# Broadcasts and output tiles in one DMA issue each, and a load order behind a gather, in an attention-plus-MLP kernel

## The chip, the core and the metric

The kernel runs on one core of one Trainium2 chip. The metric is the device time of one execution in microseconds (us); the median of several runs is compared. The engines have short names: PE is TensorE, DVE is VectorE, ACT is ScalarE, POOL is GpSimd, SP is SyncE. SP computes nothing here; it issues DMAs, one after the other, and waits on semaphores before each where it must.

## What is computed

Cosine attention for 8 batches, 12 heads, 448 positions and 64 columns per head, and then a feed-forward layer with the gate h * cos(h):

```
q_n = q / (norm(q) + 1e-06);  k_n = k / (norm(k) + 1e-06)
attn = softmax(q_n @ k_n.T / tau);  attn_out = attn @ v        # (8, 12, 448, 64)
x = attn_out, heads side by side                               # (3584, 768)
h = x @ w_in                                                   # (3584, 2048)
out = (h * cos(h)) @ w_out                                     # (3584, 768)
```

## The kernel before

**Units, pairs, batches.** The 96 heads are taken in pairs of two (48 pairs, g), three pairs make a unit (16 units, u), and two units a batch (8 batches). For each pair, q and k are loaded in float32 ("load u p", L589, two DMAs), squared, summed and normalised, scaled to bf16 (POOL, L668) and transposed, from pair 9 on by a DMA transpose ("T", L685). PE then makes the scores (L719, L727), ACT their exponentials (L734), and PE multiplies them with v and with ones (L760 to L793), so that each pair leaves unnormalised outputs and sums of exponentials.

**From sums to xT.** For pairs in the "direct" list the reciprocals are made on ACT. For the others, 34 pairs in 13 units, `chain` (L884) does it: a gather of the sums from SBUF to SBUF in two DMAs (L888), a sum and a reciprocal on 128 partitions (DVE, L900 and L903), a "spread" of the result to a scratch tensor in DRAM (L904), and a broadcast from there into RB, each half of the 128 partitions by its own DMA (L906): 64 partitions read the same row of n x 448 floats, n the number of pairs. POOL multiplies outputs by RB into xT (L910).

**The feed-forward part.** Per batch, `m1` multiplies xT (six chunks, one for each pair) by w_in in 16 steps of six matmuls (L918); ACT and DVE make h * cos(h) (L947, L949) into gT, which has room for two batches. The second product runs in 28 tiles of 128 tokens (L1016, the last ones L1045); its fills are spread between the scores of the next batch, where PE would wait for ACT. DVE copies each tile to one of three buffers osb (L983), and SP writes it to DRAM in two DMAs of 64 partitions (L987). A tile's token p of segment h goes to row `row + 7 * p`; 28 tiles over eight batches of 448 tokens make tiles 3, 10, 17 and 24 straddle two batches.

**Order.** PE's order is written out by hand: PLAN holds scripts in which `s24.2` is a block of scores, `a`, `b`, `c` the parts of attention, `f5` five fills and `m4` a block of the feed-forward part, and "given" holds the fills of some pairs. The other engines' orders come from a planner (`Program.arrange`), which plays the program with a cost for each operation and a due time, and takes what is ready and due first. `dma` gives each issue a cost and a number of descriptors from the table ISSUE (L525), and a pad, time that the planner adds after landing. "queue" in PLAN holds pairs of issues whose order on SP is fixed. Waits are set from the order found.

So an instruction waits in its engine's order for the ones before it: SP for the inputs of an issue, DVE for a gather's landing.

Of the kernel before, what the change touches and what calls it, by code (L numbers as in the profile page):

```python
# [13 lines left out]
PLAN = {  # L14
    "apart": 1,
    "ahead": (1, 2),
    "hurry": {},
    "rush": {},
    "swapped": {},
    "script": {19: """  # L20
        s19.0 f5 s19.1 f4 s19.2 f6 s19.3 f6 a18 f4 b18 s20.0 c18 c19
        s20.1 f2 a19 f2 b19 s20.2 f4 s20.3 f4 a20 s21.0 f4 s21.1 f4 b20 c20 s21.2 f6 s21.3 f6 o201 m2 c21
# [9 lines left out]
        s37.3 f4 s38.0 f4 s38.1 f4 s38.2 f4 s38.3 f4 a37 f2 b37 s39.0 c37 c38 s39.1 a38 f3 b38 f1 s39.2 f3 s39.3 f3 m5 c39  # L32
        a39 f4 s40.0 b39 f4 s40.1 f4 s40.2 f2 s40.3 f2 s41.0 s41.1 f4 s41.2 f5 s41.3 f5 a40 f2 b40 s42.0 c40 c41
        s42.1 a41 f3 b41 f1 s42.2 f4 s42.3 f4 s43.0 f4 s43.1 f4 s43.2 f5 s43.3 f5 a42 f2 b42 s44.0 c42 c43
        s44.1 f2 a43 f2 b43 s44.2 f5 s44.3 f7 a44 s45.0 f5 s45.1 f5 s45.2 f6 b44 c44 s45.3 f10 o012 m6 f6 s46.0 f12 a45 s46.1 b45 f4 c45 s46.2 f3 s46.3 f4
        """},
    "after": (0, 1, 2, 0, 1, 2, 0, 1),
    "queue": (("bcast13", "out18"), ("bcast9", "out11"), ("bcast11", "out15"),
              ("spread13", "T46"), ("spread9", "T34"), ("spread11", "T40")),
    "last": ((0,), (1,), (2,)),  # L40
    "folded": (0, 1, 2, 3),
    "grid": {2: (16, 5, 6), 3: (11, 3, 4), 4: (8, 2, 3)},
# [6 lines left out]
    "v3": (7, ("xa", 2, 0)),  # L49
    "late4": {2: (7, "T9")},  # L50
    "power": (2,),
    "late": 0.5,
    "mixed": (3, (3, 0, 1, 2, 0, 1, 2, 0), (2, 3, 4, 0, 1, 5)),
    "turned": 9,
    "first": (3, 1, 2, 0, 3, 1, 2, 0),
# [14 lines left out]
    "u5": ("gather2", "gather2", "gather2"),  # L70
    "tail": 192,
    "twin": 4,
    "given": {13:(0,0,2,3),16: (4, 0, 5, 2), 22:(1,2,5,6), 34: (12, 4, 5, 6), 46: (12, 4, 3, 4), 47: (4, 0, 5, 0)},
    "roots": (3, (14, 0), (10, 0)),
    "lead": {33: 5, 45: 6, 12: 13, 21: 13},
    "vloads": {3: [(4, "x6"), (5, "x6")], 4: [(6, "x11")], 5: [], 6: [(7, "x15"), (8, "x15")]},
# [338 lines left out]
def bass_cosine_attention__then__act_gcu_kernel(  # L415
# [9 lines left out]
    B, NH, S, D = q.shape  # L425
    DM = NH * D
# [3 lines left out]
    UH = 2 * UP  # L430
    NG = UP * NU
    PB = NG // B
    NB = 7
    NT3 = NB // 2
    BP = S // NB
# [23 lines left out]
    def sbs(name, n, shape, dt):  # L459
        return [sb("%s%d" % (name, i), shape, dt) for i in range(n)]  # L460

    def ps(name, shape, dt):
# [20 lines left out]
    osb = sbs("osb", 3, [128, DM], F32)  # L483
# [12 lines left out]
    scr = nc.dram_tensor("scr", (NU, UH * S), F32)  # L496
# [11 lines left out]
    RBv = [t.ap().rearrange("p (g s) -> p g s", g=UP) for t in RB]  # L508
# [13 lines left out]
    MH = HW / 2400.0 + 0.0025  # L522
    HALF = 0.096

    ISSUE = {"load": (0.62, 128), "gather": (0.64, 128), "spread": (0.4, 128), "bcast": (0.62, 64),  # L525
             "out": (0.62, 64), "T": (1.27, 1024)}

    def dma(eng, fns, reads, writes, sem, bulk=0.0, label="", behind=None, weight=1.0, pad=0.0):
        took, descs = 0.75, 0
        for y in ISSUE if eng == "SP" else ():  # L530
            if label.startswith(y):
                took, descs = ISSUE[y]
        o = P.op(eng, lambda e: [f(e) for f in fns], reads, writes, cost=took * len(fns), dma=sem, bulk=bulk, label=label)
        o.nd, o.descs, o.lead = len(fns), descs * len(fns), 0.3 if label[0] == "T" else 0.0
        o.weight, o.pad = weight, pad
        if behind is not None:
            P.order_only(behind, o)
        return o
# [3 lines left out]
    def act(fn, reads, writes, cols, table=None, aps=0, label="", bias=0.0):  # L542
        o = P.op("ACT", fn, reads, writes, cost=0.165 + cols / 1200.0 + 0.09 * aps, label=label, bias=bias)
        if table is not None:
            if last_table[0] is not None:
                P.order_only(last_table[0], o)
            last_table[1].append(o)
        return o
# [9 lines left out]
    def dve(fn, reads, writes, cycles, lock=False, label="", bias=0.0):  # L558
        return P.op("DVE", fn, reads, writes, cost=0.15 + cycles / 960.0, lock=lock, label=label, bias=bias)

    def pool(fn, reads, writes, cost, label="", bias=0.0):
        return P.op("POOL", fn, reads, writes, cost=cost, lock=True, label=label, bias=bias)
# [321 lines left out]
    def chain(u):  # L884
        i, b = u % 2, u // 2
        n = sum(UP * u + p not in PLAN["direct"] for p in range(UP))
        w = SPR // UP * n
        dma("SP", [lambda e, r=r: e.dma_start(  # L888
            sums[i].ap()[:, w * r : w * r + w],
            bass.AP(xu, (32 * r * 5 + 3 + i) * UP * S, [[64 * 5 * UP * S, 2], [w, 64], [1, w]]))  # L890
            for r in range(2)], [("xs", i, p) for p in range(n)], [("sums", i)], "sums%d" % i, 0.7,
            "gather%d" % u, pad=0.0 if u in PLAN["power"] else PLAN["late"])
        r = rcp[i].ap()[:, 0:w]
        parts = sums[i].ap()[:, 0 : 2 * w].rearrange("p (r x) -> p r x", r=2)
        if u in PLAN["power"]:
            pool(lambda e: e.tensor_tensor(r, parts[:, 0], parts[:, 1], ALU.add), [("sums", i)], [("rcp", i)], 0.23, label="sum")
            pool(lambda e: e.tensor_tensor(r, r, bass.AP(cst, 2, [[4, 128], [0, w]]), ALU.pow), [("rcp", i), "cst2"], [("rcp", i)],
                 0.05 + 0.166 * w, label="recip")
        else:
            dve(lambda e: e.tensor_reduce(out=r, in_=sums[i].ap()[:, 0 : 2 * w].rearrange("p (r x) -> p x r", r=2),  # L900
                                          axis=mybir.AxisListType.X, op=ALU.add), [("sums", i)], [("rcp", i)], 2 * w,
                label="sum", bias=PLAN["rush"].get(u, 0.0))
            dve(lambda e: e.reciprocal(r, r), [("rcp", i)], [("rcp", i)], 8 * w, label="recip", bias=PLAN["rush"].get(u, 0.0))  # L903
        dma("SP", [lambda e: e.dma_start(bass.AP(scr, u * UH * S, [[w, 128], [1, w]]), r)],  # L904
            [("rcp", i)], [("scr", u)], "scr", 0.02, "spread%d" % u).bias = PLAN["hurry"].get(u, 0.0)
        dma("SP", [lambda e, a=a: e.dma_start(  # L906
            RBv[i][64 * a : 64 * a + 64, 0:n], bass.AP(scr, u * UH * S + a * n * S, [[0, 64], [1, n * S]])) for a in range(2)],
            [("scr", u)], [("RB", i, p) for p in range(n)], "RB%d" % i, 3.4 * n / UP, "bcast%d" % u, None, 2.4, 0.5).bias = PLAN["hurry"].get(u, 0.0)
        for p in range(n):
            pool(lambda e, p=p: e.tensor_tensor(xTv[b % 2][:, UP * i + p, :], xuv[:, u % 3, p, :], RBv[i][:, p, :], ALU.mult),  # L910
                 [("RB", i, p), ("xa", u % 3, p)], [("xT", b % 2, UP * i + p)], 1.1, label="x%d" % (UP * u + p))
# [42 lines left out]
    def segments(t):  # L954
        segs = []
        for h in range(2):
            x = 128 * t + BP * h
            segs.append((BP * h, x // S * S + x % S // BP))
        return segs
# [17 lines left out]
    def m2_drain(t, hf, name, po, w):  # L977
        o, n, ends = t % 3, w[1] - w[0], t == B * S // 128 - 1
        dst, keys = osb[o].ap()[:, w[0] : w[1]], [("osb", o, y) for y in range(2)]
        if ends and w[1] == DM:  # L980
            act(lambda e: e.activation(dst, po[:, 0:n], ACT.Copy, bias=0.0), name + [("osb", o, 0)], [("osb", o, hf)], n, label="osb%d" % t)
        else:
            dve(lambda e: e.tensor_copy(dst, po[:, 0:n]), name, [("osb", o, hf)], n, label="osb%d" % t)  # L983
        if not ends and hf == 0:
            return
        c0, c1 = w if ends else (0, DM)
        fns = [lambda e, p0=p0, row=row: e.dma_start(  # L987
            bass.AP(out.tensor, row * DM + c0, [[NB * DM, BP], [1, c1 - c0]]), osb[o].ap()[p0 : p0 + BP, c0:c1]) for p0, row in segments(t)]
        for x, eng in enumerate(("SP", "ACT") if ends and hf else ("SP",)):
            dma(eng, fns[x : x + 1] if ends and hf else fns, [("osb", o, hf)] if ends else keys, [], "last" if x else "out%d" % o,  # L990
                n / DM if ends else 1.0, "out%d" % t, None, 1.0)

    def gates(t, f, m):
        par = sorted({(x // S) % 2 for x in (128 * t, 128 * t + 127)})
# [139 lines left out]
    def unit_done(g):  # L1134
        u = g // UP
        if g > PB and not direct(g - 1) and (g % UP == 0 or direct(g)):
            chain((g - 1) // UP)
        if g % UP == 0:
            if g > PB and (u <= 3 or u % 2 == 0):
                for x in range(UP if u + 2 < NU else 0):  # L1140
                    load(u + 2, x, x + 1, behind=find("bcast%d" % (2 if u == 4 else u - 1)) if u > 3 else
                         find(PLAN["u5"][x]) if u == 3 else None)
            if g > PB:
                for x, y in PLAN["vloads"].get(u, [(u + 2, "x%d" % (g - 1 if u % 2 == 0 else g - 4))]):
                    load_v(x, find(y))
# [156 lines left out]
    if not direct(NG - 1):  # L1302
        chain(NU - 1)
# [47 lines left out]
```

## Time and profile before

| what | us |
|---|---|
| median of 3 runs (range) | 421.33 (420.74 to 423.37) |
| the profiled execution | 421.37 |
| its span, first to last instruction | 419.6 |
| PE busy in the span | 410.8 |
| SP's issues of broadcasts (L906), first to last start | 79.2 to 370.8 |
| median landing of a 336 KB broadcast DMA, from its issue | 4.8 |
| median landing of a 192 KB output DMA, from its issue | 3.6 |
| granted PE clock | 1.000 |

The span counts from the first instruction, and all places in time below are microseconds from it. A row of the profile's groups names line, engine, operation and tiles, output before input. A wait is put down to what ended it. In windows, the columns after the five engines' busy times are the granted clock, the DMA share (the mean busy share of the core's 16 DMA engines) and GB/s. DMA packets moved 63.61 MB in the span, most of it in the first two thirds.

### The profile page before, as it was taken

To read this page: it belongs to the slowest core of one execution; us is meant where nothing else is said; L and a number is where in the kernel's file an instruction comes from. 1 tells how busy PE (TensorE), PEld (TensorE's weight loads), DVE (VectorE), ACT (ScalarE), POOL (GpSimd) and SP (SyncE) were. 2 spreads that over 40 slices of the span, in tenths; PEclk is the share of its full clock that TensorE was granted. 3 is DMA by queue.
4 is the path that set the end of the run, shared out by engine and by line. 5 is a ranking of instruction groups with operands and counts; after the bars stand their busy time and mean duration, and the time that the engine had idled before them with its cause. 6 is when DMAs were issued, how large, how long until landed. Compare 5 with 4: busy or idle time off the path is not lost.

```text
span 419.6 us, 13577 instructions
## 1 busy us (share of the span) xinstructions
PE 410.8 (98%) x6077; PEld 237.0 (56%) x6077; DVE 189.1 (45%) x250; ACT 271.9 (65%) x363; POOL 242.7 (58%) x193
## 2 busy tenths in 40 slices
PE   8899999999999999999999999999999999999997
PEld 3454556655556555665566555665566655565565
DVE  4564744456653277124752087213862244223421
ACT  5897578984986646877498556776498745703500
POOL 4999977989862694838864783908857320020000
PEclk9999999999999999999999999999999999999999
DMA  8999999979957998779867993969937720141023
GB/s 186 248 253 226 207 225 171 229 176 195 141 109 142 201 208 195 114 160 218 174 104 133 219 244 76 143 114 208 243 90 122 167 67 2 43 120 38 2 65 86
DMA packets 80254, 63.61 MB, mean 152 GB/s; under 512 B 44996, under 2 KB 75204, under 8 KB 80196
## 3 DMA queue, kind: packets, MB, share of 16 engines
q1 hardware_dynamic: 61988, 50.06, 56.8%
q0 software_dynamic: 18048, 12.59, 20.1%
q8 instruction: 48, 0.79, 0.8%
q10 hardware_dynamic: 160, 0.10, 0.1%
q14 instruction: 10, 0.08, 0.1%
HBM read 54.98 MB, written 11.13 MB: 158 GB/s over the span
## 4 chain that ended last, share of the span: by engine, by line
PE 84%; DMA 5%; ACT 4%; POOL 3%; DVE 2%; issue 1%; SPq 0%; ACTq 0%; DVEq 0%; POOLq 0%
PE MP L1016 25%; PE SC L918 18%; PE AV L918 10%; PE SC L719 6%; DMA sums<-xu 4%; PE AV L767 4%; PE MP L1045 4%; PE SC L1045 3%; PE AV L793 2%; ACT PX L734 2%; PE SC L767 2%; PE AV L760 2%; PE MP L918 2%; POOL qks L668 1%; ACT cosb L947 1%; DVE gT L949 1%
## 5 line engine op out<-in xcount | busy, mean ns | idle before, releaser
L734 ACT ACTIVATE PX<-SC 128x896 bf16<-128x896 f32 (+1 forms) x166 | 132.6, 828 | 25.5 <-PE SC L719 16.8
L1016 PE MATMUL MP<-W,gT 64*64 64x384 bf16 x2816 | 142.1, 323 | 0.9 <-DVE qkT L706 0.6
L1016 PEld LDWEIGHTS MP<-W,gT 64*64 64x64 bf16 x2816 | 79.0, 107 | 36.0 <-PE MP L1016 4.2
L668 POOL TENSOR_TENSOR qks<-raw,rn 128x896 bf16<-128x896 f32 (+1 forms) x48 | 79.8, 1678 | 28.5 <-ACT rn L660 27.9
L918 PE MATMUL SC<-xT,W 128*128 128x448 bf16 x468 | 94.9, 353 | 0.0
L947 ACT ACTIVATE cosb<-SC,cst 128x896 f32<-128x896 f32 x39 | 39.1, 1006 | 57.0 <-PE SC L918 55.1
L629 POOL TENSOR_TENSOR sq<-raw 128x896 bf16<-128x896 f32 x44 | 73.5, 1689 | 4.4 <-DMA raw<-in_q_dram 2.5
L910 POOL TENSOR_TENSOR xT<-xu,RB 128x448 bf16<-128x448 f32 x34 | 37.8, 1137 | 60.5 <-DMA RB<-scr 60.5
L918 PEld LDWEIGHTS SC<-xT,W 128*128 128x128 bf16 x468 | 45.5, 98 | 42.8 <-ACT xu L847 0.6
L949 DVE TENSOR_TENSOR gT<-SC,cosb 128x896 bf16<-128x896 f32 x39 | 42.3, 1088 | 37.5 <-ACT cosb L947 36.1
L918 PE MATMUL AV<-xT,W 128*128 128x448 bf16 x264 | 56.7, 353 | 0.0
L983 DVE COPY osb<-MP 128x384 f32<-128x384 f32 x50 | 25.7, 551 | 64.8 <-PE MP L1016 54.2
L636 DVE TENSOR_REDUCE n<-sq 128x14 f32<-128x896 bf16 (+2 forms) x49 | 51.2, 1057 | 5.9 <-ACT sq L627 5.2
L719 PE MATMUL SC<-qkT 64*64 64x448 bf16 x504 | 45.6, 356 | 0.6 <-ACT PX L734 0.4
L918 PEld LDWEIGHTS AV<-xT,W 128*128 128x128 bf16 x264 | 25.6, 98 | 24.2 <-ACT xu L847 0.3
L947 ACT ACTIVATE cosb<-AV,cst 128x896 f32<-128x896 f32 x22 | 22.1, 1006 | 23.6 <-PE AV L918 20.7
L949 DVE TENSOR_TENSOR gT<-AV,cosb 128x896 bf16<-128x896 f32 x22 | 23.9, 1087 | 15.2 <-ACT cosb L947 15.2
L603 POOL DMA_DIRECT2D va<-in_v_dram x32 | 21.9, 689 | 7.0 <-DMA raw<-in_q_dram 4.3
L877 POOL TENSOR_TENSOR xT<-xu,RB 128x448 bf16<-128x448 f32 x8 | 9.1, 1134 | 29.1 <-ACT RB L873 29.1
L850 DVE COPY xu<-AV 128x896 f32<-128x896 f32 x13 | 14.2, 1091 | 21.2 <-PE AV L783 14.3
L734 ACT ACTIVATE PX<-AV 128x896 bf16<-128x896 f32 (+1 forms) x26 | 21.1, 812 | 2.5 <-PE AV L719 1.7
L719 PEld LDWEIGHTS SC<-qkT 64*64 64x64 bf16 x504 | 14.5, 105 | 14.4 <-ACT PX L734 6.1
(95 smaller groups left out, 430.4 us busy)
## 6 DMA issues: line engine op xcount, KB each, us to landing
raw<-in_k_dram SPq DMA_DIRECT2D x48, 224.0 KB, 6.1
raw<-in_q_dram SPq DMA_DIRECT2D x48, 224.0 KB, 6.9
out_dram<-osb SPq DMA_DIRECT2D x54, 192.0 KB, 3.6
va<-in_v_dram POOLq DMA_DIRECT2D x32, 192.0 KB, 7.8
RB<-scr SPq DMA_DIRECT2D x18, 336.0 KB, 4.8
W<-in_moe_w_in_dram POOLq DMA_DIRECT2D x4, 768.0 KB, 14.7
W<-in_moe_w_out_dram POOLq DMA_DIRECT2D x4, 768.0 KB, 19.4
RB<-scr SPq DMA_DIRECT2D x6, 224.0 KB, 3.7
```

The costliest lines, as they stand in the source:

```text
L629: pool(lambda e, x=x, y=y: e.tensor_tensor(y, x, x, ALU.mult), src_, dst, 0.1 + n * 1.78e-3, label="sq%d.%d" % (u, p)).pad = LATE if u > 1 ...
L636: dve(lambda e, w=w: e.tensor_reduce(out=n2v[i][:, 2 * p : 2 * p + 2, w], in_=sqv[p][:, :, w, :], axis=mybir.AxisListType.X, op=ALU.add), ...
L668: f = lambda e, s0=s0, s1=s1: e.tensor_tensor(qksv[i][:, p, s0:s1].rearrange("p s h d -> p h s d"), rawv[i][:, h, s0:s1, :], bass.AP(rn[i] ...
L719: m = e.matmul(ph[BP * o : BP * o + BP, a, 0:S], t[r, c - 1 + (NT3 + 1) * o, 0:BP], t[r, :, BP : 2 * BP], start=True, stop=True)
L734: act(lambda e: e.activation(PHv[j] if c == 0 else PXv[j][:, c - 1], ph[:, :, 0:n], ACT.Exp, scale=1.0 / TAU), keys, [("PX", j, c)], 2 * n ...
L910: pool(lambda e, p=p: e.tensor_tensor(xTv[b % 2][:, UP * i + p, :], xuv[:, u % 3, p, :], RBv[i][:, p, :], ALU.mult), [("RB", i, p), ("xa", ...
L918: t = e.matmul(ph[:, a, 0:S], W1v[:, order[c], 128 * n : 128 * n + 128], xTv[b % 2][:, order[c], :], start=(c == 0), stop=(c == NKC - 1))
L947: act(lambda e, ph=ph, cz=cz: e.activation(cosv[cz], ph[:, :, 0:S], ACT.Sin, bias=cst.ap()[:, 0:1], scale=1.0), names(gi) + ["cst0"], [("c ...
L949: dve(lambda e, ph=ph, cz=cz, gi=gi: e.tensor_tensor(gTv[:, 2 * gi : 2 * gi + 2, S * (b % 2) : S * (b % 2) + S], ph[:, :, 0:S], cosv[cz], ...
L983: dve(lambda e: e.tensor_copy(dst, po[:, 0:n]), name, [("osb", o, hf)], n, label="osb%d" % t)
L1016: r = e.matmul(POH[b][x : x + 64, 0:HW], gTv[k, y, col + x : col + x + 64], W2v[k, y, HW * b : HW * b + HW], start=(y == 0 and h == 0), st ...
L1045: r = e.matmul(po[:, 0 : w[1] - w[0]], gTv[:, y, col : col + 128], W2v[:, y, w[0] : w[1]], start=(y == 0), stop=(y == NF - 1))
```

## The change

It makes one DMA of two in two places. The broadcast into RB becomes one DMA over 128 partitions, whose source names the two rows outermost. An output tile whose two segments are neighbouring rows of one batch becomes one DMA, whose destination names the two rows outermost; that holds for 23 of the 28 tiles. The planner is told of it (ISSUE, `descs`). "queue" gets three entries: the loads of unit 9 are issued after the gather of unit 6. The pad after a gather, 0.5 for all units but one, becomes 1.0, 1.2 and 1.0 for units 9, 11 and 13. Two orders of PE change by a few fills: those of pair 13, and `f12 a45` becomes `a45 f12`.

In the order that results, SP has the same issues with fewer DMAs. Gather 6 stands ahead of the six load DMAs of unit 9 and behind tile 5; tile 4 stands ahead of transpose 21 rather than behind it. On DVE, sums and reciprocals of units 6, 10, 11, and some neighbours of theirs, move by one or two places. POOL issues the load of unit 15's v six places later, behind the squares of that unit.

```diff
-        s44.1 f2 a43 f2 b43 ... m6 f6 s46.0 f12 a45 s46.1 b45 f4 c45 s46.2 f3 s46.3 f4
+        s44.1 f2 a43 f2 b43 ... m6 f6 s46.0 a45 f12 s46.1 b45 f4 c45 s46.2 f3 s46.3 f4
...
-              ("spread13", "T46"), ("spread9", "T34"), ("spread11", "T40")),
+              ("spread13", "T46"), ("spread9", "T34"), ("spread11", "T40"),
+              ("gather6", "load u9 p0"), ("gather6", "load u9 p1"), ("gather6", "load u9 p2")),
...
-    "late": 0.5,
+    "late": {9: 1.0, 11: 1.2, 13: 1.0},
...
-    "given": {13:(0,0,2,3),16: (4, 0, 5, 2), ...
+    "given": {13: (0, 0, 3, 2), 16: (4, 0, 5, 2), ...
...
-    ISSUE = {..., "bcast": (0.62, 64),
+    ISSUE = {..., "bcast": (0.62, 128),
...
-            "gather%d" % u, pad=0.0 if u in PLAN["power"] else PLAN["late"])
+            "gather%d" % u, pad=0.0 if u in PLAN["power"] else PLAN["late"].get(u, 0.5))
...
-        dma("SP", [lambda e, a=a: e.dma_start(
-            RBv[i][64 * a : 64 * a + 64, 0:n], bass.AP(scr, u * UH * S + a * n * S, [[0, 64], [1, n * S]])) for a in range(2)],
+        dma("SP", [lambda e: e.dma_start(
+            RBv[i][:, 0:n].rearrange("p g s -> p (g s)"), bass.AP(scr, u * UH * S, [[n * S, 2], [0, 64], [1, n * S]]))],
...
+        rows = [row for p0, row in segments(t)]
+        whole = not ends and rows[1] == rows[0] + 1
+        if whole:
+            fns = [lambda e: e.dma_start(bass.AP(out.tensor, rows[0] * DM, [[DM, 2], [NB * DM, BP], [1, DM]]), osb[o].ap())]
...
-                n / DM if ends else 1.0, "out%d" % t, None, 1.0)
+                n / DM if ends else 1.0, "out%d" % t, None, 1.0).descs *= 1 + whole
```

## The prediction

> **What bounds the kernel now.** I read the page first, then the list of DMA issues, the windows, SyncE's timeline, and the waits. The page says that TensorE is the bound and the DMA engines are not, though they are full in the first two thirds:
>
> ```profile
> PE 410.8 (98%) x6077; PEld 237.0 (56%) x6077; DVE 189.1 (45%) x250; ACT 271.9 (65%) x363; POOL 242.7 (58%) x193
> ...
> DMA  8999999979957998779867993969937720141023
> ```
>
> TensorE idles 8.8 us of 419.6, so shorter issues can win very little. The DMA row is a mean over 16 engines, and it hides how one transfer is spread over them. That is what this change alters. The list of DMA issues shows it (size each, median us to landing):
>
> ```profile
> out_dram<-osb SPq DMA_DIRECT2D x54, 192.0 KB, 3.6
> ...
> RB<-scr SPq DMA_DIRECT2D x18, 336.0 KB, 4.8
> ...
> sums<-xu SPq DMA_DIRECT2D x18, 10.5 KB
> scr<-rcp SPq DMA_DIRECT2D x9, 10.5 KB, 1.5
> ```
>
> Only the gathers (sums<-xu, L888) have no landing time. It is given where an issue leaves sixteen landing marks: 22 output issues left 352 marks, 14 gathers left 42, three each. The gather's source pattern has two rows outermost, [[.., 2], [w, 64], [1, w]]; all others have 64 or 128. Windows with one kind of transfer in flight say the same (last columns: granted clock, DMA share, GB/s; first the gathers of unit 15, then the broadcasts of unit 14, then output tile 20):
>
> ```profile
> 364.00:364.90 0.90, 0.90 (x24) 0.45 (x20) 0.00 (x0) 0.15 (x1) 0.00 (x0) 1.00 0.14 12
> 340.00:342.00 2.00, 2.00 (x13) 1.04 (x11) 1.48 (x2) 1.20 (x2) 0.00 (x0) 1.00 1.04 280
> 359.30:360.50 1.20, 1.20 (x38) 0.78 (x28) 0.00 (x0) 0.95 (x2) 0.00 (x0) 1.00 0.99 261
> ```
>
> A share of 0.14 of sixteen is 2.2 engines (packets overlap a little), a share of 1 is all. In the packet records the two gathers issued at 333.35 are 256 packets in exactly two chains. So a gather runs on two engines, and both gathers on the same two. Next, the path of a reciprocal, from SyncE's timeline (start, us: gather, spread, broadcasts), and who waits at its end:
>
> ```profile
> 333.35 1.19 SPq L888 DMA_DIRECT2D sums<-xu  x2
> 336.96 0.35 SPq L904 DMA_DIRECT2D scr<-rcp  x1
> 338.41 1.15 SPq L906 DMA_DIRECT2D RB<-scr  x2
> ```
> ```profile
> POOL xT L910 <- DMA RB<-scr: 60.5, 8, 13.0
> ```
>
> POOL's products feed xT, which the first matmul block of each batch reads (here blocks 2 and 3, in the chain of waits):
>
> ```profile
> 143.53 1.24 PE SC L918 x6
> ...
> 190.46 1.25 PE AV L918 x6
> ```
>
> Unit 7's broadcast landed at 189.98, and its first product ended at 191.19; block 3 wants it at 192.68. There is 1.5 us of slack. TensorE's order is fixed, so a later broadcast stops it.
>
> **The broadcast in one issue (13 times).** It removes 13 issues of 0.55 us (1.15 for two) from SyncE, which idles between its issues: worth nothing. But its source is now [[n*448, 2], [0, 64], [1, n*448]], two rows outermost, the gather's form. I take it that it runs on two engines, which then carry 64 rows of 5376 B each instead of 8. Per row the fastest tenth of the packet records took 206 ns; the quiet window gives 280/16 = 17.5 GB/s per engine, 307 ns. So a broadcast of three pairs keeps two engines for 13.2 to 19.7 us, of two (3584 B) 9.0 to 13.1, of one 4.7 to 6.6. I take the fast ends: 307 ns came with sixteen engines reading the same 5 KB, now two do. Before, issue to last landing was 5.4 us (338.41 to 343.78); alone it becomes 1.3 to the first packet + 13.2 + 0.7 = 15.2.
>
> **The output tile in one issue (23 of 28).** It also removes issue time that hides nothing. The destination is [[768, 2], [5376, 64], [1, 768]], two rows outermost, so 64 rows of 3072 B per engine: 7.7 us at the fastest tenth (121 ns), 8.1 at the median of all records (126), 12.1 at the window's 261/16 GB/s. I take 8.1. Four tiles that straddle batches and the last keep two issues.
>
> The Trainium skill, page "DMA: Bandwidth & Descriptors", section "Why a DMA increments its semaphore by 16 and not by 1", says that the hardware path looks at the slowest dimension above 1 of source and destination and uses the largest number of engines up to 16 that divides both. The gather's marks agree; for a two-row DRAM side no run here shows it. By the same page's ~27 GiB/s per engine (Specifications), an estimate of a three-pair broadcast is 11.9 us and of a tile 6.8, and the sum below would be some 45 us smaller. The section "Bandwidth" of that page says to batch into larger DMAs, which would speak for the change and gives the sixteen-engine rival's time.
>
> **The two engines as a queue.** All other DMAs of SyncE also use these two engines, and packets of a queue are served in order there. Loads, transposes, spreads and gathers therefore wait behind broadcasts and tiles. Per lane the rest costs at the fast records: a unit's loads 48 x 74 ns = 3.5 us, its v 48 x 60 ns = 2.9, a transpose 56 x 18 ns = 1.0, a pair of gathers 1.1. Where a cycle's last reciprocal path is exposed, the lane idles up to 6.4 us (338.41 - 333.35 + 1.3). Cycles run from one block's wait for its last broadcast to the next's:
> Block 2 to 3 (46.9 us of TensorE): loads of 8 and 9 7.0, v 8.7, five transposes 5.0, gathers 2.2, tiles 5 to 8 32.4, broadcasts 13.2 + 9.0, idle 6: 83.5, so +36.6.
> Block 3 to 4 (46.9): 7.0 + 5.8 + 7.0 + 2.2, tile 9 and straddling 10 9.1, 26.4, idle 5: 62.5, +15.6.
> Block 4 to 5 (49.4): 7.0 + 5.8 + 6.0 + 2.2, tiles 11 to 14 32.4, 26.4, idle 6: 85.8, +36.4.
> Block 5 to 6 (47.2): 7.0 + 5.8 + 6.0 + 2.2, tiles 15 to 17 17.2, 26.4, idle 6: 70.6, +23.4.
> Block 6 to 7 (43.4): 1.0 + 2.2, tiles 18 to 21 32.4, 13.2 + 9.0, idle 8: 65.8, +22.4.
> Up to block 2: +5 where block 1 waits for unit 2's broadcast behind tile 0, +19 where T21, spread 5 and broadcast 5 (9.0) stand behind broadcast 4 (13.2) and tile 4 (8.1): +24. End: tile 26, behind 25, lands some 6 us later: +5.8.
> Sum +164.2.
>
> **Loads of unit 9 behind gather 6, pads, script.** The chain of waits has the one stall that this aims at:
>
> ```profile
> 149.04 12.90 DMA sums<-xu
> ```
>
> Gather 6, behind six loads, holds VectorE's sum, then gT, then TensorE: a 0.61 us hole in 165 to 170 (4.39 busy). Freed, it saves at most 0.6; squares of unit 9 waited only 0.40 and 0.61 for loads, so loads some 2 us later cost POOL that, and at most 0.6 reaches TensorE by the same route. The loads, tile 6, spread 6 and broadcast 6 queue behind the gather's wait on SyncE, whose inputs are done at 143.2. New pads move a few sums in VectorE's order by one or two places of 1.09 us, beside TensorE. POOL issues unit 15's v six operations later (1.34 us of issue, from 294.8 to about 304), and 7.8 us of landing leave over 40 us to its first use at 355.5. The swapped fills change order, not work. Together -0.6 to +0.6, taken as 0; the other term covers them.
>
> The profiled execution took 421.37 us, its span 419.6, the median of three 421.33, so 421.4 + 164 = 586.
>
> **Rivals.** (1) Two engines, but slow packets: 4.0 us more per tile (23) and 6.5 per three-pair broadcast (9), 4 per two-pair (3): +162 where all is exposed, some 740. For it: the median 5376 B record is 353 ns; against: fourteen engines are then idle. (2) Only the broadcasts shrink to two engines, because their small dimension is at the source like the gather's, and the tiles' is at the destination, which no row tests. Tiles then cost the lane 1.0: cycles of 55, 55, 57, 56 give +8, +8, +8, +9, with +10 before block 2 and +3 at block 7: 467. (3) The other side, no slower: a DRAM side is split over all sixteen engines whatever its form. Then bytes and packets are as before, and only the 0.6 us hole goes: 420.8. It decides if the issues show sixteen landing marks. Against: the gather. Faster by over 1% needs 4.2 us, half of all of TensorE's idle time, for which no mechanism is in sight.
>
> **Numbers.** Two engines at near the fast rates 0.75, slow packets 0.12, broadcasts alone 0.07, sixteen engines 0.06. Prediction 586. The likeliest case: not below 525, since from tile 0's issue (77.5) the lane has 150 of broadcasts, 178 of tiles and 119 of the rest at the fastest records, with no idle time; up to 660. I give 525 to 700, for part of the slow packets. One per cent, 4.2 us, is about what a measurement of this kernel can tell from no change: slower 0.94, within 0.05, faster 0.01.
>
> **What would show it.** The lists of DMA issues lose the landing times of RB<-scr and of whole tiles; a window with one broadcast alone has a share near 0.13 and 30 to 52 GB/s. POOL's wait for RB<-scr grows from 60 us to well over 100, TensorE's busy share falls to about 70%, with holes ahead of each L918 block and of scores whose transposes are late. Sixteen engines in those windows, or DMA shares near 1, would make the forecast wrong outright; tiles with landing times but broadcasts without mean rival 2.

## The result, and the profile after

| | us |
|---|---|
| changed kernel, median of 5 runs (range) | 624.72 (619.37 to 627.21) |
| kernel before, median of 5 runs (range) | 421.47 (420.74 to 423.37) |
| ratio, with its 95% interval | 1.4797 [1.4763, 1.4831] |
| profiled execution of the changed kernel, and its span | 627.21, 625.3 |
| forecast, and its range | 586, 525 to 700 |

The changed kernel takes half as long again. Line numbers are one higher than before, and five higher behind the output tiles (broadcast L907, first products of a block L919, tiles in two issues L988, in one L993, second product L1021). The page of the changed kernel, with the rows of TensorE, its granted clock and the DMA engines:

```profile
PE 449.1 (72%) x6077; PEld 249.2 (40%) x6077; DVE 188.9 (30%) x250; ACT 274.4 (44%) x363; POOL 242.5 (39%) x193
...
PEclk9999997879679786969779977696977986996898
DMA  9999939899196499597949819559993291111012
```

TensorE idles 176.2 us of the span, where it idled 8.8. Two things are new beside that: the granted clock is no longer full, and the same 6077 products keep TensorE busy for 38.3 us longer. The list of DMA issues, from the same page:

```profile
out_dram<-osb SPq DMA_DIRECT2D x23, 384.0 KB
...
RB<-scr SPq DMA_DIRECT2D x9, 672.0 KB
...
out_dram<-osb SPq DMA_DIRECT2D x8, 192.0 KB
```

Both merged transfers have lost their landing time, as the gathers always lacked it: they leave three landing marks an issue, not sixteen. The eight issues of tiles that straddle batches have lost it too, only because they count on the same semaphores: on one of these, seven merged tiles and eight unmerged issues left 149 marks, 7 x 3 + 8 x 16. Windows with one broadcast alone in flight, and then one tile alone (last columns: granted clock, DMA share, GB/s):

```profile
158.00:162.00 4.00, 0.00 (x0) 0.00 (x0) 0.00 (x0) 0.00 (x0) 0.00 (x0) 1.00 0.13 54
166.00:171.00 5.00, 0.00 (x0) 0.00 (x0) 0.00 (x0) 0.00 (x0) 2.52 (x3) 0.50 0.13 52
```

A share of 0.13 is two engines of sixteen. But for three operations of POOL, nothing else runs in these stretches, TensorE included, and fourteen DMA engines stand idle. The packet records give the rate: 206 ns for a packet of 5376 B (median; 353 before) and 121 ns for one of 3072 B (126 before). The path of unit 14's reciprocals, in SyncE's timeline (start, us held: gather, spread, broadcast), and the wait at its end:

```profile
509.77 9.07 SPq L889 DMA_DIRECT2D sums<-xu  x2
523.57 0.34 SPq L905 DMA_DIRECT2D scr<-rcp  x1
525.02 0.53 SPq L907 DMA_DIRECT2D RB<-scr  x1
```
```profile
POOL xT L911 <- DMA RB<-scr: 239.4, 13, 33.5
```

From the gather to the broadcast's issue it was 5.1 us and is 15.3. SyncE itself is held at issues, which I read as the two engines' queue being full: here 9.07 us for two gathers (1.19 before), 15.58 us for a transpose at 493.45. POOL's wait for broadcasts has grown from 60.5 to 239.4 us.

The cycles from one block's wait for its last broadcast to the next's, in the same terms as the forecast (us):

| stretch | before | after | longer by | forecast |
|---|---|---|---|---|
| to block 1 | 88.2 | 95.1 | 6.9 | 5 |
| block 1 to 2 | 57.5 | 93.5 | 36.0 | 19 |
| 2 to 3 | 46.9 | 84.0 | 37.1 | 36.6 |
| 3 to 4 | 46.9 | 70.7 | 23.8 | 15.6 |
| 4 to 5 | 49.4 | 87.5 | 38.1 | 36.4 |
| 5 to 6 | 47.2 | 76.5 | 29.2 | 23.4 |
| 6 to 7 | 43.4 | 68.6 | 25.3 | 22.4 |
| 7 to the end | 39.9 | 49.4 | 9.5 | 5.8 |
| sum | | | 205.7 | 164.2 |

### The profile page after: what moved, and what is told of

Read it like the earlier page. It is cut to its first block, busy times and chain, and to the rows that moved or that the text cites. A ratio compares the mean times of both kernels' runs of the same rounds, so it can differ in the third digit from the quotient of the medians.

```text
span 625.3 us, 13541 instructions
## 1 busy us (share of the span) xinstructions
PE 449.1 (72%) x6077; PEld 249.2 (40%) x6077; DVE 188.9 (30%) x250; ACT 274.4 (44%) x363; POOL 242.5 (39%) x193
## 4 chain that ended last, share of the span: by engine, by line
PE 34%; DMA 31%; issue 11%; SPq 9%; POOL 7%; ACT 3%; DVE 2%; POOLq 0%; ACTq 0%; DVEq 0%
DMA sums<-xu 9%; DMA RB<-scr 8%; PE SC L919 8%; PE MP L1021 7%; DMA qkT<-qks 7%; PE AV L919 6%; DMA scr<-rcp 4%; SPq L686 4%; POOL qks L669 4%; SPq L590 3%; DMA raw<-in_q_dram 2%; PE SC L720 2%; PE AV L768 2%; PE MP L1050 2%; POOL xT L911 1%
## 5 line engine op out<-in xcount | busy, mean ns | idle before, releaser
L1021 PE MATMUL MP<-W,gT 64*64 64x384 bf16 x2816 | 153.9, 342 | 3.3 <-issue 1.6
L911 POOL TENSOR_TENSOR xT<-xu,RB 128x448 bf16<-128x448 f32 x34 | 37.6, 1129 | 239.4 <-DMA RB<-scr 239.4
L919 PE MATMUL SC<-xT,W 128*128 128x448 bf16 x468 | 102.9, 372 | 27.6 <-POOL xT L911 27.6
L1021 PEld LDWEIGHTS MP<-W,gT 64*64 64x64 bf16 x2816 | 85.4, 113 | 43.5 <-issue 7.3
L669 POOL TENSOR_TENSOR qks<-raw,rn 128x896 bf16<-128x896 f32 (+1 forms) x48 | 79.6, 1676 | 36.4 <-ACT rn L661 35.8
L919 PE MATMUL AV<-xT,W 128*128 128x448 bf16 x264 | 65.3, 390 | 33.4 <-DVE gT L950 18.2
L919 PEld LDWEIGHTS SC<-xT,W 128*128 128x128 bf16 x468 | 47.2, 102 | 77.4 <-POOL xT L911 30.5
L720 PE MATMUL SC<-qkT 64*64 64x448 bf16 x504 | 49.2, 378 | 8.5 <-issue 7.9
L919 PEld LDWEIGHTS AV<-xT,W 128*128 128x128 bf16 x264 | 27.5, 106 | 64.2 <-issue 28.1
L728 PE MATMUL SC<-qkT 64*64 64x224 bf16 x160 | 11.6, 274 | 39.9 <-DMA qkT<-qks 33.5
L720 PEld LDWEIGHTS SC<-qkT 64*64 64x64 bf16 x504 | 15.9, 111 | 23.4 <-issue 12.9
L901 DVE TENSOR_REDUCE rcp<-sums 128x21 f32<-128x42 f32 (+1 forms) x12 | 2.3, 194 | 74.0 <-DMA sums<-xu 74.0
## 6 DMA issues: line engine op xcount, KB each, us to landing
W<-in_moe_w_in_dram POOLq DMA_DIRECT2D x4, 768.0 KB, 14.8
```

Of the source, the lines that this page charges most:

```text
L669: f = lambda e, s0=s0, s1=s1: e.tensor_tensor(qksv[i][:, p, s0:s1].rearrange("p s h d -> p h s d"), rawv[i][:, h, s0:s1, :], bass.AP(rn[i] ...
L720: m = e.matmul(ph[BP * o : BP * o + BP, a, 0:S], t[r, c - 1 + (NT3 + 1) * o, 0:BP], t[r, :, BP : 2 * BP], start=True, stop=True)
L919: t = e.matmul(ph[:, a, 0:S], W1v[:, order[c], 128 * n : 128 * n + 128], xTv[b % 2][:, order[c], :], start=(c == 0), stop=(c == NKC - 1))
L1021: r = e.matmul(POH[b][x : x + 64, 0:HW], gTv[k, y, col + x : col + x + 64], W2v[k, y, HW * b : HW * b + HW], start=(y == 0 and h == 0), st ...
```

## The experiments

The theory: a transfer whose outermost dimension counts two rows is carried by two DMA engines, and these two become the queue for everything. The rivals: that one issue in place of two costs the time, whatever engines carry it; that the moved loads do; and, for the 41 us that the forecast missed, the halved clock.

**Which part of the change.** Two kernels have one merging each, in the order of the changed kernel. `tiles_one`:

```diff
...
-            RBv[i][:, 0:n]..., bass.AP(scr, u * UH * S, [[n * S, 2], [0, 64], [1, n * S]]))],
+            RBv[i][64 * a : 64 * a + 64, 0:n], bass.AP(scr, u * UH * S + a * n * S, [[0, 64], [1, n * S]])) for a in range(2)],
```

> Only the output tiles are merged; the broadcasts go back to two issues of 64 copies each; order of the work as in the changed kernel. Two-engine theory (a transfer whose outermost dimension counts two rows is spread over two DMA engines): a merged tile is 64 packets of 3072 B on each of two engines, at 121 ns 7.7 us, and a broadcast, spread over sixteen again, is waited for only until its share on those two engines has come through behind the tiles (about three tiles to a block: up to 23 us, of which the changed order hides a good part). Estimate 480 us, 450 to 510; the tiles leave no landing of their own in the list of DMA issues, the broadcasts do again; the wait for RB<-scr falls from 239 us to under 150. Rival, the merging as such (one issue for two halves holds back what the first half alone would release, whatever engines carry it): the tiles release only the output buffers, which were never waited for, so 421 to 430 us. Rival, the moved loads and gather: as the changed kernel, 620 us or more.

`bcast_one`:

```diff
-        whole = not ends and rows[1] == rows[0] + 1
+        whole = False
```

> Only the broadcasts are merged; the output tiles go back to two issues; order of the work as in the changed kernel. Two-engine theory: a broadcast is 64 packets of 5376 B on each of two engines, at 206 ns 13.2 us, where it took some 3 us; what it adds is 6 to 10 us at each of six blocks, since nothing long stands ahead of it on those engines. Estimate 470 us, 455 to 485; the two parts alone then add less (about 50 and 60 us) than both together (205 us), since together they queue on the same two engines. Merging as such: the scaling has to wait for both halves of a broadcast, 1 to 2 us at each of six blocks, 425 to 435 us. Moved loads and gather: 620 us or more.

Measured: merged tiles alone 516.07 us (514.57 to 517.53), ratio 1.2229 [1.22, 1.2259]; merged broadcasts alone 525.62 (524.5 to 527.68), 1.246 [1.2424, 1.2496]. So the parts cost 94 and 104 us, and both together 203: they add up, where I had expected about half of it from the parts. Both estimates were too low, and so was rival 2 of the forecast (467) by 59 us. TensorE's waits in the kernel with merged broadcasts show where:

```profile
PE SC L728 <- DMA qkT<-qks: 22.3, 3, 8.5
PE SC L919 <- POOL xT L911: 21.6, 4, 10.3
PE AV L728 <- DMA qkT<-qks: 9.2, 1, 9.2
PE AV L776 <- issue: 8.7, 1, 8.7
PE AV L784 <- issue: 7.6, 1, 7.6
```

For that case I had added up what the two engines carry (55 to 57 us a cycle). The cycles measured are 64.6, 62.9, 73.7 and 70.7. A single broadcast of 13.2 us is a wait of its own, for POOL's products at its end, for each transpose issued behind it, and for something else that the lines call "issue" (below), even where the engines are idle later in the cycle. A sum of loads bounds a cycle from below only.

**The rest of the change.** `rest_only` applies both of the diffs above; `loads_only` is the kernel before with three entries more:

```diff
-              ("spread13", "T46"), ("spread9", "T34"), ("spread11", "T40")),
+              ("spread13", "T46"), ("spread9", "T34"), ("spread11", "T40"),
+              ("gather6", "load u9 p0"), ("gather6", "load u9 p1"), ("gather6", "load u9 p2")),
```

> Both back to two issues; what is left of the change is the move of the loads of unit 9 behind the gather of unit 6 and the order that goes with it. Two-engine theory: the move alone is worth -0.6 to +0.6 us, 420.8 to 421.9 us; TensorE's granted clock stays at full from 7 us on and the wait for RB<-scr is near 60 us again. Theory that the moved loads and gather carry the loss: above 500 us.

> The kernel before with one part of the change alone: the loads of unit 9 are issued behind the gather of unit 6 (three entries of queue); pads, fills, broadcasts and tiles as before. If the stall at the gather was what the order change won (ratio 0.9974 with everything but the merging): the 0.6 us hole of TensorE at 165.6 is gone, 0.997 to 0.999 of the time before. If the win came from the pads and fills: 1.000, within 0.001.

Measured: `rest_only` 420.99 us (420.13 to 421.94), ratio 0.9974 [0.9958, 0.999]; `loads_only` 421.64 (420.83 to 422.7), 0.999 [0.997, 1.0011]. The window of the hole, in the kernel before, in `rest_only` and in `loads_only` (after the width of 5 us: TensorE's busy time):

```profile
165.00:170.00 5.00, 4.39 (x104) 3.08 (x108) 2.41 (x3) 3.67 (x7) 4.82 (x3) 1.00 1.06 168
```
```profile
165.00:170.00 5.00, 4.96 (x124) 3.16 (x116) 2.28 (x3) 4.49 (x9) 4.57 (x3) 1.00 0.90 178
```
```profile
165.00:170.00 5.00, 4.96 (x124) 3.12 (x120) 2.18 (x3) 4.49 (x8) 4.90 (x3) 1.00 0.98 187
```

The hole is filled by the move of the loads alone: 4.39 us busy become 4.96 in five. Its 0.6 us are too few to be told from nothing in the times (0.999, up to 1.0011). The order with pads and fills as well is faster by 0.1 to 0.4%, and is the fastest version of this study. Whether the pads and fills add to it stays open.

**How many engines, or how many issues.** `one_issue_16` keeps one issue for each transfer but names 128 rows outermost (and merges 27 tiles, not 23):

```diff
-            ..., bass.AP(scr, u * UH * S, [[n * S, 2], [0, 64], [1, n * S]]))],
+            ..., bass.AP(scr, u * UH * S, [[0, 128], [1, n * S]]))],
...
-            fns = [... [[DM, 2], [NB * DM, BP], [1, DM]]), osb[o].ap())]
+            fns = [... bass.AP(out.tensor, 128 * t * DM, [[DM, 128], [1, DM]]), osb[o].ap())]
```

> One issue for each broadcast and each tile as in the changed kernel, and the same bytes, but addressed with 128 rows outermost instead of two: the broadcast hands row 0 of its pair to both halves (the second half is scaled with the wrong reciprocals), and a tile's 128 rows go to 128 rows of the output that follow each other (an order of rows that is not the reference's). Two-engine theory: 128 rows are spread over sixteen engines, so about 421 us (417 to 426), and broadcasts and tiles show landings in the list of DMA issues again. Theory that one issue in place of two costs the time, however it is addressed: near 620 us. If packets of a broadcast that all read one row are slower than those of two rows, the time lies between, under 440 us.

`bcast_two_2lanes` does the opposite for the broadcasts, with the tiles in two issues, and `four_lanes` the same with 4 x 16:

```diff
...
+        dma("SP", [lambda e, a=a: e.dma_start(
+            RBv[i][64 * a : 64 * a + 64, 0:n].rearrange("p g s -> p (g s)"),
+            bass.AP(scr, u * UH * S + a * n * S, [[0, 2], [0, 32], [1, n * S]])) for a in range(2)],
...
```

`four_lanes` also writes the destination of each half of the 23 tiles as 4 x 16 rows, in place of 64:

```diff
-            bass.AP(out.tensor, row * DM + c0, [[NB * DM, BP], [1, c1 - c0]]), ...
+            bass.AP(out.tensor, row * DM + c0, ... [[16 * NB * DM, 4], [NB * DM, 16], [1, DM]]), ...
```

> Tiles in two issues, broadcasts in two issues of 64 partitions each, as before the change, but the source of each half is addressed as 2 x 32 copies of its row ([[0, 2], [0, 32], [1, n*448]]) instead of 64. Same values, same bytes, same packets. Two-engine theory: each half goes to two DMA engines, and both halves to the same two, so the time is that of the kernel with merged broadcasts alone, 525 us (515 to 535), the wait for RB<-scr near 176 us. Theory that the loss comes from one issue in place of two: as before the change, 420 to 424 us.

> As the run with 2 x 32 copies, but 4 x 16 copies for each half. Two-engine theory carried on: four DMA engines with 32 packets of 5376 B each, 6.6 us at 206 ns where two take 13.2 and sixteen 1.6. Scaled by the time beyond sixteen engines, (6.6 - 1.6) / (13.2 - 1.6) of the 104 us that merged broadcasts cost, the loss is 45 us: 466 us, and less where TensorE hides a part: 435 to 470. If a source of more than two rows outermost is spread over all sixteen: 421 us. If not the spread but the form as such costs: 525 us.

Measured: one issue on 128 rows 423.16 us (420.92 to 424.26), ratio 1.0024 [1.0003, 1.0045]; two issues of 2 x 32 copies 548.14 (544.24 to 553.63), 1.2901 [1.2866, 1.2935], above the 515 to 535 expected; 4 x 16 copies 471.6 (470.44 to 478.25), 1.1158 [1.1123, 1.1193], just above the 435 to 470 expected. In the first the landings are back:

```profile
out_dram<-osb SPq DMA_DIRECT2D x27, 384.0 KB, 4.0
...
RB<-scr SPq DMA_DIRECT2D x9, 672.0 KB, 4.4
```

Against `rest_only` (420.99), which has the same order in two issues, the one issue on 128 rows is 2.2 us slower, so the saved issues win nothing even on sixteen engines. The outermost count decides: broadcasts with two rows cost 104 us and more, with four rows 49 (45 by scaling). In `four_lanes` they leave five landing marks an issue, but the tiles leave sixteen and land in 4.4 us:

```profile
out_dram<-osb SPq DMA_DIRECT2D x54, 192.0 KB, 4.4
...
RB<-scr SPq DMA_DIRECT2D x18, 336.0 KB
```

So it is the count that reaches the DMA, not the one in the kernel's text. The trace has each of these tile issues as 64 rows: the 4 x 16 rows follow each other in equal steps, and were joined somewhere on the way. The 49 us are therefore the broadcasts' alone. Why the 4 x 16 copies of one row weren't joined, no run here shows. The Trainium skill, page "DMA: Bandwidth & Descriptors", section "Why a DMA increments its semaphore by 16 and not by 1", has the rule that the slowest dimension above 1 sets how many engines a transfer uses; these runs agree for two, four and 128, on a DRAM source and (with two and 128) a DRAM destination. One number stays open: two issues of 2 x 32 cost 22.5 us more than one issue on the same two engines. A packet of 5376 B takes 274 ns there on average, 233 in `bcast_one`; over 576 packets for each engine (nine broadcasts of 64) that is 23.6 us, about the difference. The median is 206 ns in both, so some packets are slowed, not all. What slows them wasn't tried. In `bcast_one` the two engines read different rows, here they read the same one; but in `one_issue_16` sixteen engines read one row, with a median of 211 ns, so one row for all is not slow as such.

**Is it the order within SyncE's queue?** `tiles_act` is `tiles_one` with the 23 merged tiles issued from ScalarE at the places of the plan:

```diff
+    for o in P.ops:
+        if o.eng == "SP" and o.label.startswith("out") and o.nd == 1 and int(o.label[3:]) < B * S // 128 - 1:
+            o.eng = "ACT"
...
```

> The kernel with merged tiles alone (516 us), but the 23 merged tiles are issued from ScalarE's queue instead of SyncE's, at the same places of the plan; the two engines carry the same packets. Theory that the loss is the order within SyncE's queue (transposes, gathers and broadcasts stand behind a tile's 64 packets, and SyncE itself is held while the two engines' queue is full): a tile on another queue no longer holds them, each packet waits for one of the tile's at most, and most of the 95 us goes: 430 to 465 us. Theory that it is the two engines' throughput: 505 to 520 us. The 23 issues cost ScalarE some 14 us, which is off the path.

Measured: 517.06 us (515.37 to 517.66), ratio 1.2237 [1.2208, 1.2266], the same as from SyncE's queue. My theory of the order fell. SyncE's timeline shows its two gathers of unit 6 held although no tile is in its own queue; tiles 5 and 6 had been issued from ScalarE at 154.97 and 161.37:

```profile
158.03 1.34 SPq L686 DMA_TRANSPOSE qkT<-qks  x1
159.47 11.90 SPq L889 DMA_DIRECT2D sums<-xu  x2
171.42 8.96 SPq L590 DMA_DIRECT2D raw<-in_k_dram  x1
```

The packet records say how the two queues share. Packets started in 2 us each:

```
from    3072 B, ScalarE's queue    84 B (gather), SyncE's queue
173     23                         3
175     22                         20
177     23                         23
179     22                         22
181     7                          65
183     0                          123
```

The two queues take turns on the two engines, one record of each after the other. The Trainium skill, page "DMA: Bandwidth & Descriptors", section "Issuing engines are not separate DMA queues", says that DMAs from different engines run on the same 16 DMA engines and interleave, and that another issuer saves only the time of the issue; 516.1 against 517.1 us agrees. I had the taking of turns right, and counted wrong: a pair of gathers has 128 packets for each engine, and each waits for one of a tile's, 2 us / 11 = 0.18 us a turn. Many small packets that take turns with large ones are about as late as if they stood behind them all.

**The clock.** In the changed kernel TensorE's clock record reads 0.5 in sixteen stretches of 3.4 to 17.1 us up to its last product, 164 us together; before, it reads 1.0 from 7.3 us to the end. The first 3.4 us of block 3, before and after:

```profile
192.68:196.08 3.40, 3.40 (x19) 1.76 (x18) 0.27 (x1) 1.89 (x3) 3.40 (x4) 1.00 1.18 169
```
```profile
272.60:276.00 3.40, 3.36 (x10) 1.36 (x11) 0.00 (x0) 0.00 (x0) 3.40 (x4) 0.50 0.51 122
```

Ten products in the time of nineteen: the clock matters to the work that it covers. Whether it matters to the total, two kernels ask, with products of zeros ahead of nine waits:

```diff
...
+    WARM_M, WARM_S = {3: 48, 4: 22, 5: 44, 6: 16, 7: 48}, {24: 58, 34: 22, 36: 72, 43: 50}
+    def busy(e, ph, n):
+        for x in range(n):
+            m = e.matmul(ph[:, 0, 0:S], zt.ap()[:, 0:128], zt.ap(), start=True, stop=True)
+        return m
...
```

> The changed kernel plus matrix products of zeros on TensorE (16 to 72 of them, 448 columns, results overwritten) just ahead of nine of its long waits from 230 us on; every other instruction keeps its place. They fill part of the idle time, so that TensorE's granted clock should stay at full there. In the changed kernel the clock record shows 0.5 in sixteen stretches after such waits, 164 us together, 123 of them from 230 us on, and TensorE's busy time is 449.1 us against 410.8. Theory that this clock is a loss of its own, added to the waits: 123/164 of the 38.3 us come back, 29 us, so 590 to 603 us. Theory that the two DMA engines set every cycle and TensorE's slower work runs beside them: 615 to 630 us, with longer waits in place of slower products.

> As the run with products of zeros before nine waits, but 36 of them instead of 72 ahead of the scores of pair 36, where they ran on for 10.7 us after transpose 36 had landed (24.6 us for 72, at the halved clock). Theory that the two DMA engines set every cycle: the cycle from block 4 to 5 falls from 96.8 us back to the changed kernel's 87.5, all cycles agree with the changed kernel's within 1.5 us, total 619 to 627 us. Theory that the halved clock is a loss of its own: 590 to 610 us.

Measured: 631.29 us (630.63 to 635.64), ratio 1.497 [1.4915, 1.5025], and with 36 ahead of pair 36 636.93 (634.04 to 639.14), 1.5094 [1.5026, 1.5161]. Both totals lie above what either theory gave, and they can't be read, since zeros ran past what they were to fill. In both kernels those ahead of pair 34 waited for the same product of VectorE (gT) as its scores, filled nothing, and put 5.9 and 7.1 us ahead of them. Those ahead of pair 36 ended 10.7 and 4.2 us after its transpose had landed, with a stop of 9.0 and 7.8 us among them of the kind told below (so the 24.6 us that the expectation gives to 72 products aren't the clock alone). In the second, those ahead of pair 43 began 14 us later in their cycle, behind two such stops, and ended 13.2 us after the transpose. The cycles without an overrun can be read (us; changed kernel, first, second): 2 to 3 84.0, 85.0, 83.1; 3 to 4 70.7, 70.8, 69.1; 5 to 6 76.5 and, in the first, 75.8; 6 to 7 68.6, 69.9, 69.4; 7 to the end 49.4, 46.8, 46.8. The cycle from 2 to 3 in the changed kernel and in the first of the two:

```profile
188.60:272.60 84.00, 51.47 (x748) 27.93 (x748) 20.60 (x27) 34.00 (x43) 31.64 (x27) 0.83 0.82 100
```
```profile
188.60:272.60 84.00, 72.50 (x854) 38.33 (x854) 20.73 (x27) 33.90 (x43) 30.69 (x27) 0.92 0.86 99
```

Halved clock covers 13 us of this cycle (84.0 x 0.08 x 2) in place of 29, and the cycle is no shorter. From 5 to 6, by the clock record, 22 us at half rate become 7, and the cycle is 0.7 us shorter. So in these four cycles slower products mostly fill what would be waiting; that the two DMA engines set the time there fits, and is argued. At the end, where products bound again, a warm TensorE wins 2.6 us. The other cycles aren't shown.

**The waits called "issue".** They needed no run of their own. In the changed kernel TensorE stops twice in the middle of a run of products that have no wait, and once ahead of scores whose wait for ScalarE had been over for 6.8 us (its waits, then its timeline around the first):

```profile
PE AV L776 <- issue: 16.4, 1, 16.4
PE SC L768 <- issue: 10.8, 1, 10.8
PE SC L720 <- issue: 7.9, 1, 7.9
```
```profile
156.40 0.36 PE L776 MATMUL AV<-PX,ones 128*32 128x448 bf16 x3
173.13 0.53 PE L776 MATMUL AV<-PX,ones 128*32 128x448 bf16 x1 [16.37 <-issue]
```

I counted TensorE's records (products, weight loads and its few semaphore records) up to each stop of over 0.9 us of this kind, from 60 us on:

| kernel | stops after record |
|---|---|
| before, `rest_only`, `loads_only`, `one_issue_16` | none |
| changed | 4033, 6337, 6593, 9665 |
| `bcast_one` | 3009, 4033, 10689 |
| `tiles_one` | 10689 |
| `bcast_two_2lanes` | 4033, 10689 |
| `four_lanes` | 4033, 8129, 10689 |
| `tiles_act` | 8385 |
| `after_warm` | 4033, 6593, 6849, 8641 |
| `after_warm2` | 4033, 6593, 6849, 8641, 10177, 10433 |

Every one of them leaves 193 when divided by 256. The page has a queue of its own for code:

```profile
q8 instruction: 48, 0.79, 0.5%
```

These are 48 packets of 16,384 B for TensorE's 12,271 records, one for every 256. So I take the place of the stops for the end of a packet of code. The products of zeros bear out that the place counts, and not the instruction: with 212 records put in ahead, record 6593 is another instruction (scores of pair 29 in place of products of pair 29), and the stop is still after record 6593. The stops of 16.4 and 10.8 us end 0.75 and 0.72 us after the last packet of a tile (172.38) and of a broadcast (312.41) on the two engines. That code is delivered behind these transfers is my reading of it; no run took it apart, and the records of the code packets don't settle it: the last one before the first stop runs from 150.91 to 152.13, and the next begins at 174.17, 1.0 us after the stop.

## Why the prediction was right, and where it wasn't

- **Two engines for each merged transfer**: right, and its rates with it: 206 ns were taken for a packet of 5376 B and 126 for one of 3072 B, and the medians are 206 and 121. But the mean of a 5376 B packet is 231 ns, so a broadcast of three pairs holds the two engines 14.8 us, not 13.2. Its marks came as described: no landing times, shares of 0.13, POOL's wait of 239.4 us ("well over 100"), TensorE 72% busy ("about 70%").
- **The issues that are saved win nothing**: right; with sixteen engines the merged issues give 1.0024, and 2.2 us more than the same order in two issues.
- **Loads of unit 9 behind gather 6, -0.6 to +0.6**: right in place and size for the loads (the hole is gone). Without the mergings the whole of it is 0.1 to 0.4% faster. In the changed kernel none of that is left, since gather 6 stands behind two-engine transfers.
- **The walk by cycles**: 2 to 3, 4 to 5 and 6 to 7 within 3 us. That is in part luck: by the packet times the broadcasts held the two engines some 25 us from 2 to 3 and 31 from 4 to 5, where the walk has 22.2 and 26.4, so other terms of it were too large. It was 17.0 short from block 1 to 2, 8.2 from 3 to 4, 5.8 from 5 to 6, 3.7 at the end, and 41 in all with what is left.
- **Up to block 2, the term mis-sized most**: "+19 where T21, spread 5 and broadcast 5 (9.0) stand behind broadcast 4 (13.2) and tile 4 (8.1)". They did: T21 was held for 13.32 us and landed at 173.73. But TensorE was stopped at record 4033 until 173.13 as well, and reached T21's scores only 5.5 us after T21 had landed; so 5.5 us came on top. And between block 1 and broadcast 4 the walk had nothing: transpose 13 was issued at 99.20, since POOL makes its input in order behind the product that waits for broadcast 2, then was held for 10.51 us by tiles 1 and 2. It landed at 119.81, 92.5 before. That made a hole of 3.7 us ahead of pair 13's scores. Another of 5.6 us follows: by the chain of waits it stands behind a load that SyncE could issue only at 110.61, after that hold, and behind POOL's squares and VectorE's gT. The text had named what queues on SyncE; of POOL's own order it said nothing. The last 2.2 of the 17.0 us stay open.
- **Block 3 to 4**: the stop at record 6593, 302.29 to 313.13, covers a wait for transpose 31 (landed at 313.73), whose scores TensorE reached 5.8 us later. The other 2.4 us, and the 5.8 us from block 5 to 6, aren't settled. From 5 to 6 lies the stop of 7.9 us at record 9665, but the first kernel with zeros has no such stop there, and its cycle is only 0.7 us shorter.
- **The end**: 2.6 of the missing 3.7 us are the halved clock in the last block.
- **What it left out altogether**: the clock. By the Trainium skill, page "TensorE: Matmul & The Clock Gate", Part 1, TensorE falls to half rate after an idle window of about 3.4 us; the stretches here are multiples of that length, so the trace agrees. The penalty of the same page, section "Terms", time at half rate times one half, would be an estimate of 82 us for 164. The runs bear that out for none of the four cycles between blocks that they could test (at most 1.6 us shorter); in the last block, where 6.0 us at half rate went, they show 2.6.
- **Rival 2** was mis-sized by 59 us (467 against 525.6), for the reason given with `bcast_one`: it added up the load of the two engines and left out that each broadcast of 13.2 us is waited for. **Rival 1**'s terms add up to 748, not 740, from which nothing follows.

## What to carry to other kernels

Before two DMAs become one, read the outermost count of both access patterns: it decides how many DMA engines carry the transfer, as long as its dimensions aren't joined into fewer on the way, and a merged pattern of two rows here cost 94 us for the tiles and 104 for the broadcasts, while the issues that it saved were worth nothing. In a profile, a DMA share of 0.13 while everything waits tells it, or a row of the list of DMA issues without a landing time (unless the row only shares its semaphore with such a transfer). To price such a queue, add up what it carries for a lower bound, and then follow each engine's own order for what stands behind a single long transfer.

## What the runs showed of the hardware that I had not expected

- TensorE stopped for 16.4 us in the changed kernel, and for up to 16.7 in others, where the profile shows no wait or one long over. All stops over 0.9 us of this kind lie a whole number of 256 records apart; that its code was late is not shown.
- A destination written as 4 x 16 rows in equal steps ran as 64 rows on sixteen engines; a source of 4 x 16 copies of one row ran on four.
- Two queues on one DMA engine take turns packet by packet, 0.18 us for a turn of 3072 B and 84 B, and SyncE was held at an issue for 11.9 us while the long transfers were ScalarE's.
- Two engines that read rows of their own took 206 ns for a 5376 B packet, where sixteen in the kernel before took 353 (medians); two that read the same row had the same median, and a mean of 274 against 233.
- The clock: one halved stretch after each long wait, in lengths of 3.4, 6.8, 10.2, 13.7 and 17.1 us, and half the products in it.
